# Cosine attention and a mixer MLP: score groups of three key chunks across pair borders, and three shared two-bank PSUM tiles

## The chip, the cores and the metric

The kernel runs on one core of a Trainium2 chip. The core has five engines that work side by side, each taking its own instructions in order: PE (the tensor engine; its weight loads are counted apart as PEld), ACT (activations), DVE (vector work), POOL (element work in on-chip memory, and the issue of some transfers) and SP (the issue of most transfers). Matmul results land in PSUM, which has eight banks of 512 fp32 columns on each of 128 partitions; ACT or DVE must move them out ("evict" them) before the place is used again. The metric is the device time of one execution in microseconds (us).

## The reference

Inputs are q, k and v of shape (8, 12, 448, 64): 8 batches, 12 heads, 448 tokens, 64 numbers a head.

```
q_n = q / (norm(q) + 1e-6);  k_n = k / (norm(k) + 1e-6)
scores = q_n @ k_n^T / tau                  # tau = 0.1
attn = softmax(scores)                      # over the keys
x = (attn @ v), heads side by side          # (8, 448, 768)
h = relu(x^T @ w_tok1) @ w_tok2             # 448 -> 256 -> 448, over tokens
u = x + h^T
out = u + relu(u @ w_ch1) @ w_ch2           # 768 -> 1536 -> 768, over channels
```

## The kernel before

The unit of the attention is a **pair** of heads; a batch has 6 pairs and the whole input 48, numbered i = 0 to 47. Keys are cut in 4 chunks of 112. For a pair the kernel does, in this order:

- `load_qk`, `load_v`: loads issued by SP, up to seven pairs ahead.
- `square`, `sums`, `norms`, `scale`: inverse norms of q and k and their product. Squares and products run on POOL (lines 187 and 221), the sums on DVE (L198, 1.2 us each), the logarithms and exponentials that make the inverse norm on ACT (L209 to L213). Later in the run `norms` is called once for three pairs.
- `tpose` (pairs 0 to 11, on PE, evicted by DVE at L237) or `tpose_dma` (pairs 12 and up, a transposing DMA from SP, L242): the transposed q and k, `qk`.
- `score(i, c)`: for key chunk c two matmuls (L256), one per head, each with 64 rows and 448 columns; the two heads lie on different halves of the array's rows and run together. They write the two banks of a tile `psS`, and ACT takes the exponential of both into `pt` (L258, 0.91 us).
- `pv(i, hh)`: 16 matmuls (L272) of `pt` with v and a column of ones into `psO`; DVE makes the reciprocal (L275) and the product `x` (L276).
- `tok1`: 8 matmuls (L285) into `psR`, Relu on DVE into `rt` (L288). `tok2`: 8 matmuls (L299) into `psU`, on DVE the sum with x as `u16` (L302). The transposed `ut` follows by a transposing DMA (L305), or on PE (`upose`, `psT`, L311).

When a batch's six pairs are through, its channel MLP is done in **units**, fed one by one between the steps of the next batches' pairs:

- `m_ch1(b, ct)`, 12 a batch: 6 matmuls (L321) of 448 columns into `psG`, evicted with a Relu by ACT into `gt` (L324).
- `m_ch2(b, m, dh)`: 12 matmuls (L336) of 384 columns into `psF`, evicted by DVE, which adds u into `ost` (L340). There are 6 or 8 units in a batch: three or four blocks of tokens m, two halves dh of the output columns. For m = 3 two additions of 64 partitions each evict a unit. After dh = 1 SP issues the output's transfers (L353, L359).

PSUM before: the pool `ps` has four tiles of one bank each, tag "b", used in turn by psO, psR, psU, psT, pst (of `tpose`), psG, psF and the warming matmuls; the pool `ps2` has two tiles of two banks for psS alone. `pts` are two buffers of `pt`, for even and odd pairs.

The order of each engine's work is the order in which the program writes it (`tc.manual_schedule`). The start (pairs 0 to 6) is written out by hand, with `warm(n)` calls of n small matmuls (L249) that only keep PE running. From pair 7 on, one turn of the loop is: two score chunks of pair i; side work for later pairs; some units; `pv` of pair i - 1; loads; some units; the other two chunks of pair i; units; `tok1` of i - 1; units; `tok2` of i - 1. `feed` takes units off the queue by a budget made of estimated PE times (`ns`), shared over what is left of the batch.

The framework puts in the semaphore waits: an instruction waits until what it reads is written and what it overwrites is read.

Of the kernel before, what the change touches and what calls it, by code (L numbers as in the profile page):

```python
# [22 lines left out]
def kernel(  # L23
# [12 lines left out]
    nc = tc.nc  # L36
# [45 lines left out]
    ps = ctx.enter_context(tc.tile_pool(name="ps", bufs=4, space=bass.MemoryType.PSUM))  # L82
    ps2 = ctx.enter_context(tc.tile_pool(name="ps2", bufs=2, space=bass.MemoryType.PSUM))
# [52 lines left out]
    for i in range(2):  # L136
        pt = cst.tile([SC, 8 * S + 64], FP16, name=f"pt{i}")
        nc.gpsimd.memset(pt[:, 8 * S:8 * S + 64], 0.0)
        pts.append(pt)
# [40 lines left out]
    def square(i, a, act=False):  # L180
        if "sq" not in pipe[i]:
            pipe[i]["sq"] = nrm.tile([SC, 2, 2 * NCH, E], FP32, name=f"sq_{i}", tag="sq")
        src = side(i, a).rearrange("p g c e -> p (g c) e")
# [5 lines left out]
    def side(i, a):  # L189
        return pipe[i]["kq"[a]][:]  # L190
# [24 lines left out]
    def scale(i, a, eng=None):  # L215
# [5 lines left out]
        (eng or nc.gpsimd).tensor_tensor(out=st["kqn"][:, a].rearrange("p c g e -> p g c e"), in0=side(i, a),  # L221
# [23 lines left out]
    def warm(n):  # L245
        if "warm" not in pipe:
            pipe["warm"] = ps.tile([128, 128], FP32, name="warm", tag="b")
        for _ in range(n):
            nc.tensor.matmul(pipe["warm"][:], id16[:], id16[:], start=True, stop=True)  # L249

    def score(i, c):
# [6 lines left out]
        nc.scalar.activation(out=pts[i % 2][:, 2 * S * c:2 * S * (c + 1)].rearrange("p (h s) -> p h s", h=2),  # L258
                             in_=psS[0:SC, :, 0:S], func=AF.Exp, scale=inv_tau)

    def pv(i, hh):
# [7 lines left out]
        for m, lo in enumerate(windows(b)):  # L269
            for c in range(NCH):  # L270
                at = (2 * c + hh) * S + lo
                nc.tensor.matmul(psO[:, m, 0:E + 1], pts[i % 2][:, at:at + 128],  # L272
                                 vt[:, g, c, 0:E + 1], start=(c == 0), stop=(c == NCH - 1))
# [5 lines left out]
    def tok1(i):  # L279
        st = pipe[i]  # L280
        w1 = (0, 1, 2, 3) if (i // NPAIR) % 2 == 0 else (4, 0, 1, 2)
        psR = ps.tile([128, TT, 128], FP32, name=f"psR_{i}", tag="b")
# [7 lines left out]
    def tok2(i, pe=False):  # L290
# [5 lines left out]
        psU = ps.tile([128, 4, 128], FP32, name=f"psU_{i}", tag="b")  # L296
# [17 lines left out]
    def m_ch1(b, ct):  # L314
# [4 lines left out]
        psG = ps.tile([128, S], FP32, name=f"psG_{b}_{ct}", tag="b")  # L319
        for dt in range(DT):  # L320
            nc.tensor.matmul(psG[:], wc1t[:, dt, ct * 128:(ct + 1) * 128],  # L321
                             ut[b][:, dt].rearrange("p m s -> p (m s)")[:, lo:lo + S],
                             start=(dt == 0), stop=(dt == DT - 1))
        nc.scalar.activation(out=gt[:, ct, (b % 2) * S:(b % 2 + 1) * S], in_=psG[:], func=AF.Relu)  # L324

    ost = {}

    def m_ch2(b, m, dh):
        gt = gts[b // 2]
        lo = 384 if m == 3 else 128 * m + (b % 2) * 512  # L330
        if dh == 0:
            ost[0] = outp.tile([128, D], FP32, name=f"ost_{b}_{m}", tag="ost")
        o = ost[0]
        psF = ps.tile([128, DH], FP32, name=f"psF_{b}_{m}_{dh}", tag="b")
        for ct in range(CT):
            nc.tensor.matmul(psF[:], gt[:, ct, lo:lo + 128], wc2t[:, ct, dh * DH:(dh + 1) * DH],  # L336
                             start=(ct == 0), stop=(ct == CT - 1))

        def add(p0, p1, bb, slot):
            nc.vector.tensor_tensor(out=o[p0:p1, dh * DH:(dh + 1) * DH].rearrange("p (j e) -> p j e", j=3),  # L340
                                    in0=psF[p0:p1].rearrange("p (j e) -> p j e", j=3),
                                    in1=u16[bb][p0:p1, 3 * dh:3 * dh + 3, slot], op=ALU.add)

        if m < 3:
            add(0, 128, b, m + b % 2)
        else:
            add(0, 64, b - 1, 3)
            add(64, 128, b, 0)
        if dh == 1:
            if m < 3:  # L350
                r = 0
                for c, p0, p1 in pieces(*MAIN[m]):
                    nc.sync.dma_start(out=out[b].rearrange("(p c) d -> c p d", c=NCH)[c, p0:p1],  # L353
                                      in_=o[r:r + p1 - p0])
                    r += p1 - p0
            else:
                (c, p0, p1), = pieces(384, S)
                for bb, r in ((b - 1, 0), (b, 64)):
                    nc.sync.dma_start(out=out[bb].rearrange("(p c) d -> c p d", c=NCH)[c, p0:p1],  # L359
                                      in_=o[r:r + 64])  # L360
# [4 lines left out]
    def ch1_units(b):  # L365
        return [(ns(S, DT), lambda ct=ct: m_ch1(b, ct)) for ct in range(CT)]

    def ch2_units(b):
        return [(ns(DH, CT), lambda m=m, dh=dh: m_ch2(b, m, dh))
                for m in ((3, 0, 1, 2) if b == B - 1 else range(3 + b % 2)) for dh in range(NDH)]  # L370

    queue = []
    fed = [0.0]

    def feed(budget, least=0.0):
        fed[0] += budget
        done = 0.0
        while queue and (fed[0] > queue[0][0] / 2 or done < least):
# [3 lines left out]
            done += t  # L382
        return done
# [5 lines left out]
    with tc.manual_schedule():  # L389
# [25 lines left out]
        warm(40)  # L415
        tpose(0, 1, 2)
        warm(3)
        tpose(0, 0, 1)
        warm(5)
# [8 lines left out]
        warm(12)  # L428
# [3 lines left out]
        warm(12)  # L432
# [11 lines left out]
        for i in range(1, NP_ALL + 1):  # L444
            b, pj = i // NPAIR, i % NPAIR
            if i < NPAIR:
# [9 lines left out]
                if i >= 2:  # L456
                    tok1(i - 2)
# [8 lines left out]
                if i >= 2:  # L466
                    tok2(i - 2, pe=(i == NPAIR - 1))
                pv(i - 1, 1)
                score(i, 3)
                if i == 1:  # L470
                    warm(8)
# [14 lines left out]
            if i == NPAIR:  # L486
# [6 lines left out]
                tok1(i - 2)  # L493
# [8 lines left out]
                tok2(i - 2, pe=True)  # L502
# [4 lines left out]
            if i == NPAIR + 1:  # L507
                queue += ch1_units(b - 1)
            early = i < 12
            least = 0.0 if early else 1.0  # L510
            if pj == 0:
                if b >= 2:
# [84 lines left out]
```

## Time and profile before

| | us |
|---|---|
| median of three runs (lowest, highest) | 408.69 (408.58, 409.4) |
| the profiled execution's own time | 407.75 |
| its span, first to last instruction | 406.0 |
| PE busy | 389.1 |
| ACT busy | 240.8 |
| POOL busy | 218.5 |
| DVE busy | 206.4 |
| mean granted clock of PE | 0.982 |

A row of the profile names the source line, the engine, the operation and the tiles as written<-read. In the page's first part stand busy time, its share of the span and the number of instructions. The fourth part follows the chain of work that ended last backwards. A timeline row gives the start in us, the length in us, the engine and what it did, and in brackets the idle time before it with what ended it; equal instructions that follow each other are one row with a count. The length of a row of matmuls takes in the time until its last result is out, so the next row can start before it ends: the pace of PE is read from starts. A row of a stretch gives its bounds, its length, the busy time of the engines asked for (PE, PEld, DVE, ACT, POOL, or PE alone) with the number of instructions, the clock granted to PE as a part of full speed, the busy share of the DMA engines, and GB/s.

### The profile page before, as it was taken

What the parts mean: (1) busy time and instruction counts of PE and PEld (TensorE: products, weight loads), DVE (VectorE), ACT (ScalarE), POOL (GpSimd) and SP (SyncE); (2) the same over time, 40 slices, a digit from 0 to 9 for tenths busy, and PEclk for the clock granted to TensorE, in tenths of its full rate; (3) what the DMA queues carried; (4) which work ended last, traced back from release to release, by engine and by line L of the source; (5) the groups of instructions that cost most, each with busy time, mean ns of one, the idle gap of its engine ahead of it and who ended that gap; (6) DMA issues with size and microseconds to landing.
All of it is one profiled execution on the core that took longest, in us unless ns stands there. A gap on an engine that the chain in (4) does not pass through costs nothing.

```text
span 406.0 us, 10118 instructions
## 1 busy us (share of the span) xinstructions
PE 389.1 (96%) x4146; PEld 240.4 (59%) x4146; DVE 206.4 (51%) x441; ACT 240.8 (59%) x392; POOL 218.5 (54%) x257
## 2 busy tenths in 40 slices
PE   6978799999999999999999999999999999999995
PEld 5656566566555665656656655556655666655562
DVE  5767877655454466554555555635636345312031
ACT  5857789954676438773587437773588535521400
POOL 7797999948557480949175852949092800000000
PEclk9868999999999999999999999999999999999999
DMA  8999999978859786867759697978974433103022
GB/s 198 239 175 251 246 262 230 209 195 180 201 142 191 140 200 157 197 161 171 201 127 187 156 184 188 164 152 187 195 130 94 114 81 92 28 15 116 2 74 81
DMA packets 102590, 64.07 MB, mean 158 GB/s; under 512 B 61328, under 2 KB 98960, under 8 KB 102544
## 3 DMA queue, kind: packets, MB, share of 16 engines
q1 hardware_dynamic: 96928, 58.22, 64.0%
q0 software_dynamic: 5616, 5.21, 8.1%
q8 instruction: 32, 0.52, 0.6%
q14 instruction: 14, 0.11, 0.1%
HBM read 43.45 MB, written 11.01 MB: 134 GB/s over the span
## 4 chain that ended last, share of the span: by engine, by line
PE 87%; DMA 5%; DVE 4%; POOL 1%; issue 1%; ACT 1%; SPq 0%; DVEq 0%; POOLq 0%
PE psF L336 27%; PE psG L321 27%; PE psO L272 12%; PE psS L256 10%; PE psU L299 5%; PE psR L285 5%; DMA kf<-in_k_dram 4%; DVE ssq L198 2%; DMA qf<-in_q_dram 1%; DVE x L276 1%; PE pst L235 1%; POOL kq L221 0%; ACT sq L185 0%; DVE ost L340 0%; DVE rt L288 0%
## 5 line engine op out<-in xcount | busy, mean ns | idle before, releaser
L258 ACT ACTIVATE pt<-psS 112x896 f16<-112x896 f32 x192 | 166.2, 914 | 84.4 <-PE psS L256 84.1
L321 PE MATMUL psG<-ut,wc1t 128*128 128x448 f16 x576 | 122.4, 353 | 0.0
L336 PE MATMUL psF<-wc2t,gt 128*128 128x384 f16 x672 | 116.6, 326 | 0.0
L221 POOL TENSOR_TENSOR kq<-kf,rn 112x512 f16<-112x512 f32 x47 | 50.0, 1063 | 99.3 <-ACT rn L213 86.3
L336 PEld LDWEIGHTS <-gt 128*128 128x128 f16 x672 | 63.1, 98 | 43.4 <-issue 5.2
L340 DVE TENSOR_TENSOR ost<-psF,u 128x384 f32<-128x384 f32 (+1 forms) x64 | 35.7, 557 | 96.2 <-PE psF L336 96.0
L324 ACT ACTIVATE gt<-psG 128x448 f16<-128x448 f32 x96 | 52.3, 545 | 53.7 <-PE psG L321 53.5
L321 PEld LDWEIGHTS <-wc1t 128*128 128x128 f16 x576 | 51.3, 98 | 46.6 <-issue 8.2
L198 DVE TENSOR_REDUCE ssq<-sq 112x16 f32<-112x1024 f32 (+1 forms) x49 | 58.1, 1189 | 9.0 <-ACT sq L185 6.4
L272 PEld LDWEIGHTS <-pt 112*128 112x128 f16 x1536 | 53.5, 99 | 15.5 <-ACT gt L324 7.0
L256 PE MATMUL psS<-qk 64*128 64x448 f16 x384 | 56.2, 363 | 3.5 <-ACT pt L258 2.7
L272 PE MATMUL psO<-vt,pt 112*128 112x65 f16 x1536 | 59.3, 195 | 0.1
L302 DVE TENSOR_TENSOR u<-psU,x 128x512 f16<-128x512 f32 x48 | 33.1, 689 | 34.2 <-PE psU L299 34.2
L187 POOL TENSOR_TENSOR sq<-kf 112x512 f32<-112x512 f32 x46 | 47.7, 1037 | 3.9 <-DMA kf<-in_k_dram 3.4
L221 POOL TENSOR_TENSOR kq<-qf,rn 112x512 f16<-112x512 f32 x45 | 46.8, 1041 | 0.0
L288 DVE TENSOR_SCALAR rt<-psR 128x256 f16<-128x256 f32 x48 | 20.2, 421 | 46.8 <-PE psR L285 46.6
L276 DVE TENSOR_TENSOR x<-psO,rec 128x256 f16<-128x256 f32 x96 | 40.8, 425 | 3.3
L187 POOL TENSOR_TENSOR sq<-qf 112x512 f32<-112x512 f32 x39 | 40.5, 1037 | 0.0
L285 PE MATMUL psR<-x,w1t 128*128 128x128 f16 x384 | 29.8, 221 | 2.6 <-DVE x L276 2.6
L285 PEld LDWEIGHTS <-w1t 128*128 128x128 f16 x384 | 25.0, 99 | 11.6 <-issue 3.3
L299 PEld LDWEIGHTS <-w2t 128*128 128x128 f16 x384 | 25.9, 100 | 9.0 <-issue 2.1
L299 PE MATMUL psU<-rt,w2t 128*128 128x128 f16 x384 | 30.1, 223 | 0.4 <-DVE rt L288 0.2
(40 smaller groups left out, 156.0 us busy)
## 6 DMA issues: line engine op xcount, KB each, us to landing
qf<-in_q_dram SPq DMA_DIRECT2D x48, 224.0 KB, 3.8
kf<-in_k_dram SPq DMA_DIRECT2D x48, 224.0 KB, 3.7
vf<-in_v_dram SPq DMA_DIRECT2D x48, 224.0 KB, 3.7
out_dram<-ost SPq DMA_DIRECT2D x8, 336.0 KB, 3.1
wc1t<-in_moe_w_ch_dram POOLq DMA_DIRECT2D x4, 576.0 KB, 8.2
wc2t<-in_moe_w_ch_dram POOLq DMA_DIRECT2D x2, 1152.0 KB, 16.3
out_dram<-ost SPq DMA_DIRECT2D x8, 288.0 KB, 2.9
out_dram<-ost SPq DMA_DIRECT2D x8, 240.0 KB, 2.8
```

Of the source, the lines that this page charges most:

```text
L187: nc.gpsimd.tensor_mul(out=pipe[i]["sq"][:, a], in0=src, in1=src)
L198: nc.vector.tensor_reduce(out=half[i // HP]["ssq"][:, a0:a1, lo:lo + 2 * NCH], in_=pipe[i]["sq"][:, a0:a1], axis=AXX.X, op=ALU.add)
L221: (eng or nc.gpsimd).tensor_tensor(out=st["kqn"][:, a].rearrange("p c g e -> p g c e"), in0=side(i, a), in1=_bcast_free(rn, E), op=ALU.mult)
L256: nc.tensor.matmul(psS[:, hh, 0:S], qk[hb:hb + 64, c * SC:c * SC + 128], qk[hb:hb + 64, S:2 * S], start=True, stop=True)
L258: nc.scalar.activation(out=pts[i % 2][:, 2 * S * c:2 * S * (c + 1)].rearrange("p (h s) -> p h s", h=2), in_=psS[0:SC, :, 0:S], func=AF.Exp ...
L272: nc.tensor.matmul(psO[:, m, 0:E + 1], pts[i % 2][:, at:at + 128], vt[:, g, c, 0:E + 1], start=(c == 0), stop=(c == NCH - 1))
L276: nc.vector.tensor_tensor(out=st["x"][:, :, hh * E:(hh + 1) * E], in0=psO[:, :, 0:E], in1=_bcast_free(rec[:], E), op=ALU.mult)
L285: nc.tensor.matmul(psR[:, tt], w1t[:, w1[m], tt * 128:(tt + 1) * 128], st["x"][:, m], start=(m == 0), stop=(m == 3))
L299: nc.tensor.matmul(psU[:, m], w2t[:, tt, lo:lo + 128], st["rt"][:, tt], start=(tt == 0), stop=(tt == TT - 1))
L321: nc.tensor.matmul(psG[:], wc1t[:, dt, ct * 128:(ct + 1) * 128], ut[b][:, dt].rearrange("p m s -> p (m s)")[:, lo:lo + S], start=(dt == 0) ...
L324: nc.scalar.activation(out=gt[:, ct, (b % 2) * S:(b % 2 + 1) * S], in_=psG[:], func=AF.Relu)
L336: nc.tensor.matmul(psF[:], gt[:, ct, lo:lo + 128], wc2t[:, ct, dh * DH:(dh + 1) * DH], start=(ct == 0), stop=(ct == CT - 1))
```

## The change

From pair 7 on the key chunks of all pairs form one list that is cut in groups of three, whatever pair they belong to: a group may hold the last chunk of one pair and the first two of the next. After each group the program writes the side work of the pairs that begin in it (`side(i)`), then one of `pv`, `tok1` or `tok2` of what is ready, then `feed`, then the `tok2` and `tok1` that may follow. Eight groups make a batch; `feed` gives each an eighth of the batch's units and at least one from the second batch on. `pt` has three buffers.

PSUM becomes three two-bank tiles (`ps2`, tag "s"), shared by psS, psG and psF, and in the start by psR, psU and some warming matmuls (`wide`), and two one-bank tiles (`ps`).

A unit of the channel MLP is twice as large: `m_ch1` makes two blocks ct in the two banks of one tile (one block in batch 0), each with its own Relu after its 6 matmuls, and `m_ch2` makes both halves dh in the two banks of one tile, each with its own addition after its 12 matmuls.

In the start, `warm(12)` before `sums(2)` goes, another becomes `warm(14)`, and `warm(8)` stands at the end of each of the pairs 1 to 5 and not of pair 1 alone.

```
-    ps = ctx.enter_context(tc.tile_pool(name="ps", bufs=4, space=bass.MemoryType.PSUM))
-    ps2 = ctx.enter_context(tc.tile_pool(name="ps2", bufs=2, space=bass.MemoryType.PSUM))
+    ps = ctx.enter_context(tc.tile_pool(name="ps", bufs=2, space=bass.MemoryType.PSUM))
+    ps2 = ctx.enter_context(tc.tile_pool(name="ps2", bufs=3, space=bass.MemoryType.PSUM))
...
-    for i in range(2):
+    for i in range(3):
         pt = cst.tile([SC, 8 * S + 64], FP16, name=f"pt{i}")
...
-    def m_ch1(b, ct):
+    def m_ch1(b, ct, n):
...
-        psG = ps.tile([128, S], FP32, name=f"psG_{b}_{ct}", tag="b")
-        for dt in range(DT):
-            nc.tensor.matmul(psG[:], wc1t[:, dt, ct * 128:(ct + 1) * 128],
-                             ut[b][:, dt].rearrange("p m s -> p (m s)")[:, lo:lo + S],
-                             start=(dt == 0), stop=(dt == DT - 1))
-        nc.scalar.activation(out=gt[:, ct, (b % 2) * S:(b % 2 + 1) * S], in_=psG[:], func=AF.Relu)
+        psG = ps2.tile([128, 2, 512], FP32, name=f"psG_{b}_{ct}", tag="s")
+        for j in range(n):
+            for dt in range(DT):
+                nc.tensor.matmul(psG[:, j, 0:S], wc1t[:, dt, (ct + j) * 128:(ct + j + 1) * 128],
+                                 ut[b][:, dt].rearrange("p m s -> p (m s)")[:, lo:lo + S],
+                                 start=(dt == 0), stop=(dt == DT - 1))
+            nc.scalar.activation(out=gt[:, ct + j, (b % 2) * S:(b % 2 + 1) * S], in_=psG[:, j, 0:S], func=AF.Relu)
...
+    def m_ch2(b, m):
...
+        psF = ps2.tile([128, 2, 512], FP32, name=f"psF_{b}_{m}", tag="s")
+        def add(dh, p0, p1, bb, slot):
+            nc.vector.tensor_tensor(out=o[p0:p1, dh * DH:(dh + 1) * DH].rearrange("p (j e) -> p j e", j=3),
+                                    in0=psF[p0:p1, dh, 0:DH].rearrange("p (j e) -> p j e", j=3),
+                                    in1=u16[bb][p0:p1, 3 * dh:3 * dh + 3, slot], op=ALU.add)
+
+        for dh in range(NDH):
+            for ct in range(CT):
+                nc.tensor.matmul(psF[:, dh, 0:DH], gt[:, ct, lo:lo + 128], wc2t[:, ct, dh * DH:(dh + 1) * DH],
+                                 start=(ct == 0), stop=(ct == CT - 1))
+            if m < 3:
+                add(dh, 0, 128, b, m + b % 2)
+            else:
+                add(dh, 0, 64, b - 1, 3)
+                add(dh, 64, 128, b, 0)
...
+    def feed():
+        fed[0] += fed[1]
+        done = 0
+        while queue and (done < fed[2] or fed[0] > queue[0][0] / 2):
+            t, fn = queue.pop(0)
+            fn()
+            fed[0] -= t
+            done += 1
+
+    def refill(b):
+        while queue:
+            queue.pop(0)[1]()
+        queue.extend((ch2_units(b - 1) if 0 < b < B - 1 else []) + ch1_units(b))
+        fed[:] = [0.0, sum(t for t, _ in queue) / 8, min(b, 1)]
+        if b == B - 2:
+            queue.extend(ch2_units(b))
...
-        warm(12)
         sums(2)
         cast_v(0)
         score(0, 2)
-        warm(12)
+        warm(14)
...
-                if i == 1:
-                    warm(8)
+                warm(8)
...
+        chunks = [(i, c) for i in range(NPAIR + 1, NP_ALL) for c in range(NCH)]
+        groups = [chunks[j:j + 3] for j in range(0, len(chunks), 3)]
...
+        while u_next < NP_ALL:
+            grp = groups[g] if g < len(groups) else []
+            for i, c in grp:
+                score(i, c)
+                if c == NCH - 1:
+                    seen[i] = g
...
+            begun = [i for i, c in grp if c == 0]
+            for i in begun:
+                side(i)
+            r_ok, u_ok = p_next, r_next
+            if seen.get(p_next, g) < g:
+                pv(p_next, 0)
+                pv(p_next, 1)
+                p_next += 1
+                r_ok = p_next
+            elif r_next < p_next:
+                tok1(r_next)
+                r_next += 1
+                u_ok = r_next
+            elif u_next < r_next:
+                tok2_of(u_next)
+                u_next += 1
+            feed()
+            for i in begun:
+                if i + 1 < DMA_T0:
+                    tpose(i + 1)
+            while u_next < u_ok:
+                tok2_of(u_next)
+                u_next += 1
+            while r_next < r_ok:
+                tok1(r_next)
+                r_next += 1
+            g += 1
```

`side(i)` holds the loads, sums, norms, products, squares, transposing DMA and cast that the loop before had in each turn, in the same order among themselves.

## The prediction

> **What bounds the kernel now.** I read the page first, then busy time by stretches, the tensor engine's timeline in one steady pair, the list of waits, and the clock in short stretches.
>
> ```profile
> PE 389.1 (96%) x4146; PEld 240.4 (59%) x4146; DVE 206.4 (51%) x441; ACT 240.8 (59%) x392; POOL 218.5 (54%) x257
> ...
> PE 87%; DMA 5%; DVE 4%; POOL 1%; issue 1%; ACT 1%; SPq 0%; DVEq 0%; POOLq 0%
> ```
>
> ```profile
> 84.00:372.00 288.00, 287.89 (x3042) 173.78 (x3041) 141.08 (x304) 168.06 (x259) 145.12 (x161) 1.00 0.67 149
> ```
>
> PE holds 87% of the chain, and from 84 to 372 us it is busy 287.89 of 288.00 us at full clock. There every microsecond that PE waits or saves is a microsecond of the end. ACT, DVE and POOL have slack.
>
> ```profile
> 273.99 0.61 PE L299 MATMUL psU<-rt,w2t 128*128 128x128 f16 x8
> 274.53 0.55 PE L256 MATMUL psS<-qk 64*128 64x448 f16 x4
> 275.01 1.19 PE L272 MATMUL psO<-vt,pt 112*128 112x65 f16 x32
> 276.05 2.11 PE L336 MATMUL psF<-wc2t,gt 128*128 128x384 f16 x12
> 278.09 0.55 PE L256 MATMUL psS<-qk 64*128 64x448 f16 x4
> 278.58 0.66 PE L336 MATMUL psF<-wc2t,gt 128*128 128x384 f16 x3
> ```
>
> Read the starts. psU takes 0.54 us before a score where it takes 0.45 before anything else (the chain gives psF 1.95, and 2.04 here before a score): entering a score group costs 0.10. Four score matmuls take 0.49; two concurrent pairs of 448 columns at psG's pace (1.14/6 = 0.19) are 0.38, so leaving costs 0.11. A group costs 0.21 us whatever its length.
>
> **Part 1, longer groups (gain).** Pairs 7 to 47 have 164 chunks: 82 groups of two before, 55 of three after. 27 x 0.21 = **-5.7 us**.
>
> **Part 2, MLP units on two-bank tiles (loss).** In batches 1 to 7 each unit holds two accumulations in one tile, j = 0 and 1, and the eviction of 0 stands before the matmuls of 1. The built instruction list, each wait followed to the instruction that brings its semaphore to the value, shows what this makes: the first matmul of half 1 of every psG waits for the Relu of half 0 of the same tile, and that of every psF for the add of half 0. Before, each unit had its own bank, and the list of waits has no PE row for L321 or L336. PE takes matmuls in order, so half 1, the psU and psR behind it and the next scores wait too, and with the scores ACT's exps, which have 41% of the span to give. There are 42 such psG and 28 psF units (3 or 4 a batch; batch 0's psG stay single). The trace shows this kind of bubble in psR to rt to psU:
>
> ```profile
> 48.29 0.62 PE L285 MATMUL psR<-x,w1t 128*128 128x128 f16 x8 [1.16 <-DVE x L276]
> 48.95 0.42 DVE L288 TENSOR_SCALAR rt<-psR 128x256 f16<-128x256 f32 x1
> 49.43 0.61 PE L299 MATMUL psU<-rt,w2t 128*128 128x128 f16 x8 [0.22 <-DVE rt L288]
> ```
>
> psR stops streaming at 48.74 (0.45 after its start), DVE starts 0.21 later, and PE resumes 0.06 after its end: the eviction plus 0.27.
> - psF: add 0.557 (L340) + 0.27 = 0.83, 24 times; the four m = 3 units need two adds (1.14 for both at 339.96): 1.41. 19.9 + 5.6 = 25.5.
> - psG with ACT free: Relu 0.545 (L324) + 0.27 = 0.81. ACT is not always free: from a group's start the first exp begins at +0.41 and the next every 0.80 (two and the row after them span 1.61 from 292.07), so three hold ACT to +2.81. With the projection (1.12) between, half 0 ends at 0.68 + 1.12 + 1.14 = 2.94 and finds ACT free: 28 units, 22.7.
> - In groups that hold only psU (0.45) before the unit, half 0 ends at 2.27; Relu runs from 2.81 to 3.36: 1.15, 6 times, 6.9.
> - In groups that begin a pair i with i mod 3 = 1, the four norm activations stand ahead of the Relu:
>
> ```profile
> 293.68 0.34 ACT L209 ACTIVATE rn<-ssq,tiny 112x48 f32<-112x48 f32 x1
> ...
> 294.84 0.53 ACT L324 ACTIVATE gt<-psG 128x448 f16<-128x448 f32 x1
> ```
>
> They take 1.16, so Relu starts at 3.97, and the bubble is 3.97 + 0.55 + 0.06 - 2.94 = 1.64, 8 times, 13.1.
>
> Sum of part 2: 25.5 + 22.7 + 6.9 + 13.1 = **+68.2 us**. Bounds: the evictions' bare durations, 24 x 0.557 + 4 x 1.14 + 42 x 0.545 = 40.8, if the 0.27 shrank to nothing; above, the sum with each bubble 0.2 larger, 82. I take 68, since the bubble row is the same mechanism.
>
> The Trainium skill speaks against such a wait: "PSUM — Partial Sum Buffer", Summary, says that PSUM may be read while a matmul runs if the matmul targets a different bank. The halves lie in different banks, so by that rule part 2 would cost nothing and the sum would end near 405.7. No run here shows it, and the program's waits decide.
>
> **Part 3, shared tiles.** Scores and MLP units rotate through three tiles, so a group's third chunk needs the tile of the last unit. Where psR or psU stands between (0.45 and more), its second eviction is done. Twelve groups (third chunks of 12_0, 15_0, 18_0 and every third pair to 45_0) follow a unit directly: tile free 0.81 after the unit, chunk ready at 0.10 + 0.38 = 0.48. 12 x 0.33 = **+4.0** (0 to 8, with an exp ahead of the Relu). psO, psR and psU have two banks for four: psO follows psR by a group's 0.78, which covers the eviction (0.42 + 0.27); cost nothing, or 0.3 a pair if DVE's 1.2 us sums get ahead.
>
> **Part 4, order.** psR 47 to psU 47 now touch: one bubble, +0.7. psR 12 waits for x behind psU 11 alone: +0.5. psT, norms, casts and loads keep their order on POOL, ACT and SP; per pair the same two loads, one transposing DMA and v load, moved behind three scores. Transposed keys (3.4 us to land) are issued about two groups ahead, some 10 us: covered. kq 10 is the exception: POOL ends it at 62.7, PE would ask near 61.3, +1.4; against it the waits behind DVE's double sums (0.51 at 66.28, 0.90 at 78.37) go: net 0, +-1.4. The third pt buffer only removes a reuse; its memset on POOL stands after the identity and before weights first used at 19.8.
>
> **Part 5, start and clock.** Full or half clock changes at steps of 3.41 us:
>
> ```profile
> 19.31:22.73 3.42, 1.80 (x30) 1.00 1.14 233
> 22.73:26.14 3.41, 3.12 (x32) 0.50 0.77 161
> 26.14:29.55 3.41, 2.77 (x29) 0.50 1.16 137
> 29.55:32.97 3.42, 3.42 (x41) 0.50 1.20 254
> 32.97:36.38 3.41, 2.58 (x40) 1.00 1.29 216
> 46.62:50.03 3.41, 2.03 (x28) 1.00 1.20 275
> ```
>
> Column three is PE busy, then the clock. It falls after 1.80 of 3.42 busy, stays after 2.03, and comes back only after a full stretch. warm(8), now in pairs 1 to 5 (8 x 0.056 at full clock, beside ACT's 4.6 us a pair), fills the gap at 26.4 to 27.4, so full clock returns at 29.55, 3.4 us earlier: **-1.5** (bounds -3 and +1). The removed warm(12) lies under key loads that land at 18.84: nothing.
>
> Later, a 1.64 bubble leaves 3.41 - 1.57 = 1.84 busy, nearer the 1.80 that fell than the 2.03 that held. The stretch must hold all of it: (3.41 - 1.6)/3.41 = 0.53 of 8, and about six in ten of those, 2.5 falls at 1.7 to 3.4 us each: **+5** (0 to 27). The other bubbles leave over 2.2. "TensorE: Matmul & The Clock Gate", Part 1, lets the clock fall after an idle window of 3.4 us; no bubble here is that long, so by it this term is 0. The row above fell half busy, so I go by the row.
>
> **Sum.** -5.7 + 68.2 + 4.0 + 1.2 + 0 - 1.5 + 5 = +71.2. The profiled execution took 407.75 (span 406.0 and 1.75 around it), so 479.0; the three runs' median lies 0.94 above that execution, which makes 480 for a median.
>
> **Rivals.**
> A: the halves run through (a wait satisfied early, or not where I read it). -5.7 + 4.0 + 1.2 - 1.5 = -2.0: 406.7, faster. For it: the banks differ and DVE and ACT are 51% and 59% busy. Against: a half can't be evicted before it ends, and PE takes matmuls in order. It decides below 2.0/70 = 0.03 us a unit, where the smallest eviction takes 0.545. 4%.
> B: bubbles as short as the bare evictions, no falls of the clock: 40.8 - 2.0 = +38.8 to about +55: 447 to 463. 14%.
> C: the clock falls at most long bubbles and takes two stretches to return, or ACT's queue makes all psG bubbles like the long ones (28 x 0.83 = 23 more): 500 to 515. For it: coming back needs 3.41 us without a gap, and units bring a gap every 2 to 4. 14%.
>
> **How the numbers follow.** Forecast 480, own range 463 to 497, 68%. With the upper half of B (455 to 463) and the near end of C (to 502) that makes 80%: 455 to 502. A change within 0.2% is about what a measurement can't tell from none. Only A is not slower: faster 0.04, same 0.01, slower 0.95.
>
> **What would show it.** PE waits on the DVE add and the ACT Relu, about 70 rows of 0.8 to 1.6 us and 60 to 75 us in sum, PE busy under 87%; psS starts in groups of six matmuls 0.68 long; a wait of psS on the add or Relu of 0.3; full clock again near 29.6; stretches at half clock after pairs 16, 19, 25. If PE has no wait inside psG or psF I am wrong altogether; if the bubbles are there and the time is under 455, their size is.

## The result, and the profile after

The changed kernel takes **482.05 us** in the median (480.67 to 484.08) where the kernel before takes 409.04 on the same chip: a ratio of 1.178, with a 95% interval of 1.173 to 1.184. The prediction was 480, with 455 to 502 as its range. The profiled execution took 483.31 us, its span 481.5. An execution that took over 1.5% more than the fastest one of its kernel is left out of the ratios.

The page of the changed kernel, first the busy times, then the shares of the chain that ended last:

```profile
PE 401.0 (83%) x4168; PEld 246.0 (51%) x4168; DVE 205.7 (43%) x441; ACT 241.9 (50%) x392; POOL 218.4 (45%) x258
...
PE 62%; ACT 15%; DMA 8%; DVE 7%; POOL 4%; issue 2%; SPq 0%; POOLq 0%
```

PE has fallen from 96% to 83% busy. On the chain ACT went from 1% to 15% and DVE from 4% to 7%, though both do the same work as before: 241.9 and 205.7 us against 240.8 and 206.4. They have become what PE waits for.

The list of waits, PE alone, from 88 us to the end (waiter, what it waited for: sum, times, longest):

```profile
PE psG L321 <- ACT gt L324: 34.3, 42, 1.6
PE psF L338 <- DVE ost L332: 20.4, 28, 1.2
PE psU L298 <- DVE rt L287: 2.7, 4, 0.7
PE psS L255 <- DVE ost L332: 1.0, 6, 0.2
PE psU L298 <- DVE x L275: 0.6, 1, 0.6
```

Before, the same list had no PE row in this part of the run. The counts of the first two rows are those of the instruction list: 42 psG units and 28 psF units wait once each, 54.7 us in sum. The list leaves out idle times under 0.15 us. The idle time is counted from the modelled end of the last matmul, which lies about 0.16 after the array could have taken the next one (a psG row is 1.30 long where its pace is 1.135), so PE loses 54.7 + 70 x 0.16 = 65.9 us of its stream.

The timeline, PE and ACT, near the end, where only units are left:

```profile
442.95 0.54 ACT L324 ACTIVATE gt<-psG 128x448 f16<-128x448 f32 x1 [0.59 <-PE psG L321]
443.54 2.43 PE L321 MATMUL psG<-ut,wc1t 128*128 128x448 f16 x12 [0.63 <-ACT gt L324]
...
444.87 0.54 ACT L324 ACTIVATE gt<-psG 128x448 f16<-128x448 f32 x1 [1.38 <-PE psG L321]
446.01 0.54 ACT L324 ACTIVATE gt<-psG 128x448 f16<-128x448 f32 x1 [0.59 <-PE psG L321]
446.60 2.43 PE L321 MATMUL psG<-ut,wc1t 128*128 128x448 f16 x12 [0.63 <-ACT gt L324]
```

Each row of 12 matmuls is half 1 of one unit and half 0 of the next. It starts 0.05 after the Relu of the half before has ended, and the rows follow each other every 3.06 us where two halves take 2.27: 0.79 lost a unit. The Relu at 444.87 belongs to the first half of the row at 443.54 and runs beside its second half: PE writes another tile there and does not stop. It stops only where the tile is the same.

Where ACT has the norms of three pairs to do first, the same view shows the long form:

```profile
142.10 1.30 PE L321 MATMUL psG<-ut,wc1t 128*128 128x448 f16 x6
...
143.21 0.34 ACT L209 ACTIVATE rn<-ssq,tiny 112x48 f32<-112x48 f32 x1
...
144.23 0.24 ACT L213 ACTIVATE rn<-rn 112x48 f32<-112x48 f32 x1
144.38 0.53 ACT L324 ACTIVATE gt<-psG 128x448 f16<-128x448 f32 x1
144.95 1.29 PE L321 MATMUL psG<-ut,wc1t 128*128 128x448 f16 x6 [1.56 <-ACT gt L324]
```

The half is through at 143.24 (1.14 after its start), its Relu starts 1.14 later, behind four small activations, and PE stands for 1.56 + 0.16 = 1.72.

The stretches from 44 to 90 us hold the second loss. First the kernel before (bounds, length, busy PE, PEld, DVE, ACT, POOL, PE's clock, DMA share, GB/s):

```profile
44.00:56.00 12.00, 10.49 (x159) 7.58 (x157) 9.70 (x22) 8.54 (x16) 11.04 (x13) 1.00 1.16 283
56.00:72.00 16.00, 15.49 (x213) 9.90 (x210) 12.01 (x24) 15.03 (x34) 15.70 (x18) 1.00 1.20 219
72.00:90.00 18.00, 17.10 (x188) 10.49 (x186) 9.52 (x20) 12.66 (x24) 13.27 (x15) 1.00 1.00 216
```

and the changed kernel:

```profile
44.00:56.00 12.00, 8.95 (x102) 5.09 (x99) 6.53 (x12) 7.88 (x16) 8.32 (x10) 1.00 1.14 236
56.00:72.00 16.00, 14.17 (x172) 8.77 (x173) 8.20 (x16) 10.88 (x22) 16.00 (x17) 0.79 1.15 226
72.00:90.00 18.00, 14.86 (x179) 9.32 (x176) 9.68 (x22) 14.57 (x29) 14.78 (x17) 1.00 1.14 241
```

The changed kernel is earlier at 44 us: its first scores of pair 7 start at 44.35 where they stood at 49.97 before. Then POOL idles for 3.7 of the 12 us to 56 and is full after it, PE is busy 2.2 us less in the last stretch, and the clock is down to 0.79 in between. The list of waits of POOL in the first 100 us says what it lacked; the first row is of the kernel before, the second of the changed one:

```profile
POOL sq L187 <- DMA kf<-in_k_dram: 3.0, 2, 1.8
```

```profile
POOL sq L187 <- DMA kf<-in_k_dram: 8.6, 4, 4.7
```

To put a number on this stretch I count the PE work done by a point in time: the matmuls that have started by then, each at its steady pace (psG 0.19, psF 0.1625, psS 0.1225, those of psR, psU, psT and pst 0.056, psO 0.032 us; warming matmuls nothing). By 44 us the kernel before has done 18.5 us and the changed one 22.0; by 90 us it is 59.9 and 55.0. A lead of 3.5 became a lag of 4.9. The measure is used again below; the figures in the expectations, written from an earlier count, differ by up to 1.4.

### The profile page after: what moved, and what is told of

It is laid out like the page before. It is cut to its first block, busy times and chain, and to the rows that moved or that the text cites. A ratio compares the mean times of both kernels' runs of the same rounds, so it can differ in the third digit from the quotient of the medians.

```text
span 481.5 us, 10090 instructions
## 1 busy us (share of the span) xinstructions
PE 401.0 (83%) x4168; PEld 246.0 (51%) x4168; DVE 205.7 (43%) x441; ACT 241.9 (50%) x392; POOL 218.4 (45%) x258
## 4 chain that ended last, share of the span: by engine, by line
PE 62%; ACT 15%; DMA 8%; DVE 7%; POOL 4%; issue 2%; SPq 0%; POOLq 0%
PE psF L338 24%; PE psG L321 19%; ACT pt L257 7%; PE psO L271 7%; ACT gt L324 5%; PE psS L255 5%; DVE ost L332 5%; DMA kf<-in_k_dram 4%; PE psU L298 3%; PE psR L284 3%; DMA qf<-in_q_dram 3%; POOL kq L221 2%; POOL sq L187 2%; DMA qk<-kq 2%; ACT rn L212 1%
## 5 line engine op out<-in xcount | busy, mean ns | idle before, releaser
L257 ACT ACTIVATE pt<-psS 112x896 f16<-112x896 f32 x192 | 163.1, 916 | 114.0 <-PE psS L255 113.8
L338 PE MATMUL psF<-wc2t,gt 128*128 128x384 f16 x672 | 117.4, 326 | 20.7 <-DVE ost L332 20.4
L321 PEld LDWEIGHTS <-wc1t 128*128 128x128 f16 x576 | 54.4, 98 | 89.1 <-issue 47.0
L338 PEld LDWEIGHTS <-gt 128*128 128x128 f16 x672 | 64.5, 97 | 67.0 <-issue 27.8
L255 PE MATMUL psS<-qk 64*128 64x448 f16 x384 | 52.9, 360 | 5.1 <-DMA qk<-kq 1.4
L298 PEld LDWEIGHTS <-w2t 128*128 128x128 f16 x384 | 24.4, 98 | 14.4 <-issue 8.1
L274 DVE RECIPROCAL rec<-psO 128x4 f32<-128x4 f32 x96 | 16.8, 176 | 32.3 <-PE psO L271 32.2
## 6 DMA issues: line engine op xcount, KB each, us to landing
wc2t<-in_moe_w_ch_dram POOLq DMA_DIRECT2D x2, 1152.0 KB, 18.5
```

Source lines behind the costliest of these rows:

```text
L255: nc.tensor.matmul(psS[:, hh, 0:S], qk[hb:hb + 64, c * SC:c * SC + 128], qk[hb:hb + 64, S:2 * S], start=True, stop=True)
L257: nc.scalar.activation(out=pts[i % 3][:, 2 * S * c:2 * S * (c + 1)].rearrange("p (h s) -> p h s", h=2), in_=psS[0:SC, :, 0:S], func=AF.Exp ...
L298: nc.tensor.matmul(psU[:, m], w2t[:, tt, lo:lo + 128], st["rt"][:, tt], start=(tt == 0), stop=(tt == TT - 1))
L321: nc.tensor.matmul(psG[:, j, 0:S], wc1t[:, dt, (ct + j) * 128:(ct + j + 1) * 128], ut[b][:, dt].rearrange("p m s -> p (m s)")[:, lo:lo + S ...
L338: nc.tensor.matmul(psF[:, dh, 0:DH], gt[:, ct, lo:lo + 128], wc2t[:, ct, dh * DH:(dh + 1) * DH], start=(ct == 0), stop=(ct == CT - 1))
```

## Theories, and the experiments

Theory 1: PE waits inside a unit because its two halves share a tile, and the wait is for the tile, for as long as the eviction takes. Rivals: ACT and DVE are late whatever the tiles; or PE can't write one bank while another is read. Theory 2, for the 44 to 90 us: the earlier arrival is worth nothing, because POOL and the key loads set the pace. Rivals: the arrival is kept; or the new order of the pairs 7 to 11 alone is at fault. Theory 3, for the rest: groups of three save what they should, and steps that touch give it back.

### Own tiles for each half

```
-        psG = ps2.tile([128, 2, 512], FP32, name=f"psG_{b}_{ct}", tag="s")
         for j in range(n):
+            psG = ps2.tile([128, 2, 512], FP32, name=f"psG_{b}_{ct + j}", tag="s")
...
-        psF = ps2.tile([128, 2, 512], FP32, name=f"psF_{b}_{m}", tag="s")
         for dh in range(NDH):
+            psF = ps2.tile([128, 2, 512], FP32, name=f"psF_{b}_{m}_{dh}", tag="s")
```

> Each half of a unit gets a two-bank tile of its own from the same three, and uses one bank of it; order of the instructions, pools and groups stay as in the changed kernel. Theory (PE waits inside a unit because both halves stand in one tile, and the wait is for the tile): the 70 waits, 54.7 us of idle time and about 0.16 of drain each, 66 us in all, go, while the evictions still read one bank as PE writes another: 482 - 66 = 416 (411 to 423), no PE row of psG or psF behind the Relu or the add above 3 us in sum. Rival 1 (the evictions come too late because ACT and DVE are behind their own queues, whatever the tiles): waits of the same sum move to the reuse of one of the three tiles, over 450. Rival 2 (PE and the evicting engine can't work in two banks at once): matmuls slow down beside the evictions and the time stays over 450 without wait rows.

Measured: 418.6 us (414.55 to 421.1) over four executions; ratio to the kernel before 1.020 (1.013 to 1.027), taken over three of them with a median of 417.12, which is used below. 64.9 of the 73 us are gone. The waits of PE from 92 us on, and PE with ACT in one feed of two units:

```profile
PE psU L298 <- DVE rt L287: 2.7, 4, 0.7
PE psS L255 <- DVE ost L331: 1.0, 6, 0.2
PE psU L298 <- DVE x L275: 0.6, 1, 0.6
```

```profile
130.12 4.70 PE L321 MATMUL psG<-ut,wc1t 128*128 128x448 f16 x24
...
131.45 0.54 ACT L324 ACTIVATE gt<-psG 128x448 f16<-128x448 f32 x1
...
132.59 0.54 ACT L324 ACTIVATE gt<-psG 128x448 f16<-128x448 f32 x1 [0.59 <-PE psG L321]
133.72 0.54 ACT L324 ACTIVATE gt<-psG 128x448 f16<-128x448 f32 x1 [0.59 <-PE psG L321]
...
134.66 0.61 PE L298 MATMUL psU<-rt,w2t 128*128 128x128 f16 x8
```

Not one psG or psF wait is left. Four halves run through in 134.66 - 130.12 = 4.54, four times 1.135, while ACT reads the tiles that PE has just left. Both rivals fall: the evictions are in time, and PE writes one bank while another is read. That is the rule of "PSUM — Partial Sum Buffer", Summary, in the Trainium skill, which the prediction set against the program's waits: of the hardware this run agrees with it, and so did the kernel before, where each unit's eviction ran beside matmuls in other banks and PE had no wait in the list. But a wait that the program holds by tile costs the time all the same.

### Own tiles for psG alone

The same edit in `m_ch1` only.

> Own tiles for the halves of psG alone; psF stays as in the changed kernel. Theory: the 42 waits of psG go (34.3 us idle + 42 x 0.16 = 41.0), the 28 of psF stay (20.4 + 28 x 0.16 = 24.9): 482 - 41 = 441 (437 to 447). Rival (one of the two kinds hides behind the other, or ACT's queue moves the wait from psG to the scores): over 450, or psF waits well above 20.4.

Measured: 440.73 us (439.47 to 443.84), ratio 1.079 (1.074 to 1.084). The psG rows are gone and the psF row is the same to the digit:

```profile
PE psF L338 <- DVE ost L332: 20.4, 28, 1.2
```

So psG costs 482.05 - 440.73 = 41.3 (expected 41.0) and psF 440.73 - 417.12 = 23.6 (expected 24.9). They don't hide behind each other.

### One tile, both evictions after both halves

```
         for j in range(n):
             for dt in range(DT):
...
+        for j in range(n):
             nc.scalar.activation(out=gt[:, ct + j, (b % 2) * S:(b % 2 + 1) * S], in_=psG[:, j, 0:S], func=AF.Relu)
```

and the same for the additions in `m_ch2`.

> Both halves stay in one tile, but both evictions are written after the matmuls of both halves. Theory: no wait inside a unit (-66); the tile comes free later, by two evictions (1.1) + 0.27 = 1.37 after the unit's end where the changed kernel's was 0.81. A group's third chunk wants that tile 0.48 after the group's start: 12 groups that follow a unit directly wait 0.9, and some 35 with psU or psR between (0.45) wait 0.3 to 0.45: 10.8 + 13 = 24 instead of 2, so 482 - 66 + 22 = 438 (422 to 445). Rival (the third chunk's wait is as small as measured, 0.17, because PE enters the group later than I count): 416 to 420. Rival 2 (waits inside a unit are not by tile): no change from 482.

Measured: 433.5 us (432.74 to 435.87), ratio 1.061 (1.056 to 1.066). The waits inside a unit are gone with the tile still shared, so it is the eviction that stands between the halves that makes them. The price is paid at the third chunk of the next group:

```profile
PE psS L255 <- DVE ost L333: 8.4, 15, 1.0
PE psS L255 <- ACT gt L325: 2.9, 5, 0.6
```

The list has 20 waits of 11.3 us; five more of 0.13 to 0.14 in the same place are too short for it. Together they are 12.0, or 16.0 with 0.16 each, where I had 47 waits of 24: those behind a psU or psR are covered. They make up the 16.4 over the run with own tiles.

### One eviction twice as long

```
-            nc.scalar.activation(out=gt[:, ct + j, (b % 2) * S:(b % 2 + 1) * S], in_=psG[:, j, 0:S], func=AF.Relu)
+            for _ in range(n - j):
+                nc.scalar.activation(out=gt[:, ct + j, (b % 2) * S:(b % 2 + 1) * S], in_=psG[:, j, 0:S], func=AF.Relu)
```

> The changed kernel with the Relu of half 0 of each psG (batches 1 to 7) written twice in a row, so that this one eviction takes 1.09 us instead of 0.545. Theory (half 1 waits for the whole eviction of half 0, so the bubble is its length plus a fixed part): each of the 42 waits grows by 0.545, 22.9 in all: 482 + 23 = 505 (500 to 509), the psG waits 34.3 + 22.9 = 57 in sum, and the 28 psF waits stay at 20.4. Rival (the wait is for the first write of the tile alone, or a fixed latency, not the eviction's length): 480 to 487.

Measured: 510.84 us (508.68 to 511.97), ratio 1.248 (1.245 to 1.252).

```profile
PE psG L321 <- ACT gt L325: 58.6, 42, 2.1
PE psF L339 <- DVE ost L333: 20.4, 28, 1.2
```

The ordinary psG bubble went from 0.63 to 1.21 idle, the long one from 1.55 to 2.13: +0.58 each, 24.3 in sum where I had 22.9. The bubble is the eviction's length plus a fixed part. The rest of the 28.8 is the clock. In stretches of PE (bounds, length, busy, clock, DMA, GB/s) of this run:

```profile
234.35:237.77 3.42, 1.28 (x6) 0.92 0.48 142
237.77:241.18 3.41, 3.41 (x25) 0.58 0.49 75
...
323.10:326.51 3.41, 1.27 (x8) 1.00 0.57 158
```

Three times (the others at 265.07 and 384.54) a stretch with 1.27 to 1.39 busy is followed by one near half speed; each costs (0.08 + 0.42) x 3.41 = 1.7, so 5.1, and 24.3 + 5.1 = 29.4. The last row is one that held with as little.

### The start without the added warm(8)

With own tiles:

```
                 score(i, 3)
-                warm(8)
+                if i == 1:
+                    warm(8)
```

> The kernel with own tiles for each half (first run of this set), with the warm(8) at the ends of the pairs 2 to 5 taken out again, as before the change (pair 1 keeps it). Theory (key loads and POOL set the pace from 45 to 86 us, so PE's earlier arrival at pair 7, 44.35 instead of 49.97, is given back there): the same time as the first run of this set, within 1.5 us, with shorter waits of POOL on the key loads. Rival 1 (the earlier arrival is kept to the end): 3 to 6 us slower than the first run. Rival 2 (the early arrival does harm, by the waits that pull the clock down at 57 to 64 us): 2 to 5 us faster.

Measured: 417.74 us (416.76 to 420.56), ratio 1.023 (1.018 to 1.027): no difference from the 417.12 with it. PE has done 20.4 us of work by 44 us instead of 21.9, and 54.0 instead of 52.5 by 90 us; POOL's waits for keys fall from 10.9 to 5.9 us. The earlier arrival is given back, as theory 2 says.

### The start's warm(8) alone, in the kernel before

```
                 score(i, 3)
-                if i == 1:
-                    warm(8)
+                warm(8)
```

> The kernel before with one part of the change alone: warm(8) at the end of each of the pairs 1 to 5. Theory (from 45 to 86 us POOL and the key loads set the pace, so an earlier arrival of PE at pair 7 is given back): the time of the kernel before, -1.5 to +1 us, even where the clock stays up from 22.7 to 33. Rival (the earlier arrival, up to 5.6 us, is kept): 403 to 406.

Measured: 409.64 us (407.2 to 411.38), ratio 1.000 (0.997 to 1.004). The clock does stay up from 24 to 48 us, and the work done by 44 us rises from 18.5 to 22.4; by 90 us it is 56.8 against 59.9. The gain I had predicted for this part, -1.5, is not there.

But that the warm(8) is what keeps the clock up is not shown. The run with the weights alone (the last one below) has only the warm(8) of pair 1, and its program is that of the kernel before until the scores of pair 4 are done. Yet it held full clock where the profile of the kernel before had half, had 21.7 us of work done by 44 us, and came to pair 7 early. Its stretch, and the first scores of pair 7 in the kernel before and in that run:

```profile
22.73:26.14 3.41, 2.76 (x53) 1.00 1.08 182
```

```profile
49.97 0.61 PE L256 MATMUL psS<-qk 64*128 64x448 f16 x4
```

```profile
45.10 0.61 PE L256 MATMUL psS<-qk 64*128 64x448 f16 x4
```

So most of the lead in the profiles can be a difference between two executions of one start. The other executions of the kernel before on record have a mean clock of 0.985 to 1.0 where the profiled one has 0.982, and when they came to pair 7 is not known. What speaks for theory 2 is that the time doesn't follow the arrival: the profiled execution of the kernel before, at pair 7 by 49.97, took 407.75, the one with the weights alone, by 45.10, took 408.19, and the one with the warm(8), by 43.97, took 410.64.

### The old order for the pairs 7 to 11

With own tiles. The old turn of the loop, cut to its core, stands ahead of the groups, which begin with pair 12:

```
+        for i in range(NPAIR + 1, 12):
...
+            quota = sum(t for t, _ in queue) / (2 * NPAIR + 1 - i)
+            score(i, 0)
+            score(i, 1)
...
+            feed_by(quota * 0.22)
+            pv(i - 1, 0)
+            pv(i - 1, 1)
+            cast_v(i)
+            load_v(i + 4)
+            feed_by(quota * 0.28)
...
+            score(i, 2)
+            score(i, 3)
+            feed_by(quota * 0.25)
+            tok1(i - 1)
+            feed_by(quota * 0.25)
+            tok2(i - 1)
-        chunks = [(i, c) for i in range(NPAIR + 1, NP_ALL) for c in range(NCH)]
+        chunks = [(i, c) for i in range(12, NP_ALL) for c in range(NCH)]
```

> The kernel with own tiles for each half, with the pairs 7 to 11 written in the order of the kernel before (two chunks, side work, pv of the pair before, two chunks, tok1, tok2, with batch 0's units between by the old shares), and groups of three from pair 12 on. Counted as PE work done by 90 us, the kernel before has 59.7 us done, the changed one 53.7, the one with own tiles 51.1, though both led by 3 at 44 us. Theory (the order of the pairs 7 to 11 leaves PE with nothing to do while POOL makes the next keys; the old order has units and pv there): most of the 8.6 come back: 409 to 413, and PE busy over 14 of the 16 us from 48 to 64 us. Rival (the key loads and POOL set the pace of this stretch whatever the order): 416 to 420, PE busy under 13 of 16.

Measured: 414.69 us (412.39 to 417.92), ratio 1.014 (1.007 to 1.022), between the two ranges. The work done by 90 us came back from 52.5 to 58.9, but PE was busy 12.61 of the 16 us from 48 to 64, which is what the rival said, and POOL still waited 8.0 us for keys. Of the 6.4 us of work only 2.4 appear in the median, and the two intervals overlap. Nor is one profile enough: the changed kernel and its runs with own tiles, own tiles for psG alone, both evictions late and one eviction twice as long have the same program up to 90 us, and had 52.5 to 56.2 done by then; the old order had 58.9 here and 56.2 in the run with tok1 held back. So the order seems to matter, and the split between order and loads is not settled.

### Groups of two

With own tiles:

```
-        groups = [chunks[j:j + 3] for j in range(0, len(chunks), 3)]
+        groups = [chunks[j:j + 2] for j in range(0, len(chunks), 2)]
-        fed[:] = [0.0, sum(t for t, _ in queue) / 8, min(b, 1)]
+        fed[:] = [0.0, sum(t for t, _ in queue) / 12, min(b, 1)]
```

> The kernel with own tiles for each half, with groups of two chunks instead of three (82 groups), and each group fed a twelfth of a batch's units instead of an eighth. Theory (a group costs 0.21 us to enter and leave, whatever its length): 27 groups more cost 5.7; against it the waits of the third chunk (6 x 0.33) and the small gaps of psU and psF behind three exps (about 1.7) go: +2 over the 418.6 of groups of three, 419 to 423. Rival (what a longer group saves is all given back by its exps, which hold tiles and ACT): the same or faster, 412 to 417.

Measured: 426.93 us (424.23 to 430.04), ratio 1.044 (1.037 to 1.050): 9.8 slower than groups of three (417.12), where I had +2. The waits of PE from 92 us on:

```profile
PE psR L284 <- DVE x L275: 6.9, 8, 0.9
PE psU L298 <- DVE rt L287: 2.8, 4, 0.8
PE psO L271 <- ACT pt L257: 1.2, 5, 0.2
```

In shorter groups tok1 stands right behind its own pv: 10.9 us of waits where groups of three have 4.3. From 90 us to its last matmul this run takes 327.4 us, with 59.7 of work done before; the run with groups of three 323.3 with 52.5 done. That is 11.3 for the steady part, near the 12.3 that 27 x 0.21 and 6.6 more of listed waits make; gaps too short for the list stand in both and are not in this sum.

### tok1 held back where no pv follows

With the kernel with own tiles and the old order for the pairs 7 to 11:

```
-            while r_next < r_ok:
-                tok1(r_next)
-                r_next += 1
+            if seen.get(p_next, g + 1) <= g:
+                while r_next < r_ok:
+                    tok1(r_next)
+                    r_next += 1
```

> The kernel with own tiles and the old order for the pairs 7 to 11 (414.69), with one change of order from pair 12 on: tok1 is not written at the end of a group when the next group has no pv to do; it stands after that group's scores, a unit after it, then tok2. Before, such a group (two in eight) ran scores, psU, unit, and the next scores touched the unit. Theory (the steady stretch loses what the longer groups save because steps that need each other touch: psU behind rt 4 x 0.69, third chunk 3 x 0.46 and 6 x 0.17, and 0.16 of drain for each of 14): these 5.4 + 2.2 go, 414.7 - 7.6 = 407 (405 to 410), no PE wait from 92 us on above 0.5. Rival (the waits only move, to psR behind x or psO behind pt): 413 to 416.

Measured: 416.29 us (413.01 to 418.57), ratio 1.017 (1.014 to 1.021): no faster. The waits did go, 5.4 to 1.5 in sum, and from 90 us to the last matmul the profiled run takes the same 317.8 us as the run before it, with 2.7 us less work done beforehand. But part of the wait only moved to where the list doesn't show it: eleven times psR takes 0.70 before a unit instead of 0.45, which fits a first half that takes the tile the first exp still reads, and six score groups are followed 0.44 later. And by 90 us this run had 56.2 done where the other had 58.9, though the two programs are the same until pair 12. Its stretch from 44 to 90 us just went worse.

### Weights loaded later

In that kernel, and in the kernel before with the warm(8):

```
-                else:
+                elif i < 4:
                     weights_ch1(i - 2)
...
-            if i == 8:
+            if i in (7, 8):
+                weights_ch1(i - 5)
+            if i == 9:
                 weights_ch2()
```

> The kernel of the run before this one in the set, with 1.2 MB of weights taken out of the time before 44 us: the third and fourth parts of wc1t are loaded in the pairs 7 and 8 instead of 4 and 5, and wc2t in pair 9 instead of 8. Theory (key loads that share the DMA engines with the weights hold POOL, which waits 8.0 us for keys before 56 us, and POOL holds PE): POOL's waits on keys fall to under 4 and the time by 2 to 4 us: 403 to 406. Rival (POOL ends its work at 85 us whatever waits it had, since ACT and DVE are in its chain too): within 1 us of the run before.

Measured: 414.2 us (412.02 to 416.2), ratio 1.012 (1.009 to 1.016), 2.1 under the run before it, not the 403 to 406 of the theory. The lead does grow (39.5 us of work by 64 us, against 36.5), and then PE stands at the first transposing DMA:

```profile
PE psS L255 <- DMA qk<-kq: 6.9, 1, 6.9
```

POOL's waits for keys fell only from 8.6 to 6.6. What the transposed keys of pair 12 waited for in their turn was not tried.

> The kernel before with warm(8) in the pairs 1 to 5 (409.64) and the weights loaded later as in the run before this one in the set. Theory (key loads were the limit that took the earlier start back): 404 to 407. Rival (as there): 408.5 to 410.5.

Measured: **406.94 us** (405.99 to 409.12), ratio 0.9955 (0.9933 to 0.9977): 1.8 us faster than the kernel before, and the fastest of all. POOL waits 3.2 us for keys where the warm(8) alone had 4.9, and 60.8 us of work are done by 90 us, where the kernel before has 59.9.

The weights alone, in the kernel before without the added warm(8):

> The kernel before with the weights loaded later alone (third and fourth parts of wc1t in the pairs 7 and 8, wc2t in pair 9), without the warm(8) of the pairs 2 to 5. The two together gave 406.94, the warm(8) alone 409.64, the kernel before 408.8. Theory (the earlier start is worth something only where the keys come early enough, so both are needed): 408 to 409.5. Rival (the later weights give the whole 2.7 by themselves, PE's earlier arrival nothing): 405.5 to 407.

Measured: 409.09 us (407.56 to 410.31), ratio 0.998 (0.996 to 1.001). Neither half of the edit is a gain by itself that can be told from nothing, and both together are 0.45%. Their ratios multiply to 0.9988; the distance to 0.9955 is 0.0033, which the three intervals (together about 0.0045) allow by chance, so that each needs the other is not shown.

## Why the prediction was right, and where it was not

- **Part 2, bubbles.** Right in cause, number and size. I had 68.2; the trace has 65.9, and taking the shared tiles away gave 64.9. psF: 24 of 0.81 and 4 of 1.37 are 24.9 (25.5 predicted). psG: 31 of 0.79, 3 of 0.91 and 8 of 1.71 are 40.9 (42.7 predicted). The step that was off is the group of 1.15 behind psU alone: six were predicted, three of 0.91 came. The eight behind the norms are there, at 1.71 for 1.64.
- **Part 1, groups.** The price of a group holds: six score matmuls take 0.67 to 0.68 to the next row, four 0.48 to 0.49, and psR in front of them 0.54 for 0.45. With listed waits counted apart, groups of two cost about what 27 x 0.21 says. But the saving of 5.7 doesn't reach the end, since the same order brings the losses of the next point, 9.9.
- **Part 3 and 4.** I had 4.0 for twelve third chunks and 1.2 for psU and psR. The third chunks are right: the list has six of 0.17, and five more stand at 0.147, below what it shows. With the 0.16 that is 0.33 and 0.31 each, 3.5 in sum (the twelfth, of pair 12, waits for its transposed keys instead). One of the five is inside this row of six matmuls, 1.07 long where one without a wait is 0.74, and 1.00 from the next row where that one is 0.67:

```profile
125.95 1.07 PE L255 MATMUL psS<-qk 64*128 64x448 f16 x6
```

  The step that failed is the other one: five psU waits are 3.3 (4.1 with the 0.16) where I had 1.2. To these come gaps that I had at nothing: psU to the unit behind it 0.64 or more for 0.45 nine times, and psU 0.06 later behind a group of three eight times, 2.3. Together 9.9 instead of 5.2.
- **Part 5, start.** Here the working failed, twice over. I expected the clock to come back 3.4 us sooner and to keep 1.5. In fact it never fell at 22.73, and PE came to pair 7 5.6 us sooner; and none of it was kept. First, I took the fall in one profile of the kernel before for a fixed part of its time: the run with the weights alone had no fall there without any added warm(8). Second, I carried a gain on PE before 44 us to the end, while in the next stretch POOL waits for the key loads, and PE for POOL. By 90 us the changed kernel is 4.9 us behind, where I had 1.5 ahead. The runs without and with the warm(8) show no difference in either kernel; that the order of the pairs 7 to 11 makes the lag is supported by the work done at 90 us (56.2 and 58.9 with the old order, 52.5 to 56.2 with the new) and not shown.
- **Part 5, clock.** Predicted +5 for falls behind the long bubbles. There were none: PE has full clock from 88 us on. The rule that I drew from two rows, that a stretch falls at 1.80 busy and holds at 2.03, put 1.84 on the wrong side. The changed kernel has six stretches with 1.85 to 1.89 busy, all at full clock; two of them:

```profile
142.20:145.61 3.41, 1.85 (x12) 1.00 0.68 161
...
196.81:200.22 3.41, 1.86 (x23) 1.00 0.66 172
```

- **The sum.** The profiled execution is 75.6 above the one before (483.31 - 407.75), and I had 71.2. The misses are -2.3 (bubbles), +6.4 (start), -5 (clock), +4.7 (parts 3 and 4), 3.8 in sum of the 4.4; the 0.6 left over are not traced. So the large term was right, and that the 480 is good to half a per cent is luck: the errors of the small terms went against each other.
- **What would show it.** Of the signs that I named, the 70 rows, their sum (with the 0.16), PE under 87% and the score groups of 0.68 are there. The third chunk's wait of 0.3 is there eleven times of twelve. Two signs are false: the clock has no return near 29.6 because it never fell there, and no half-clock stretches stand after pairs 16, 19 and 25.
- **The rivals.** A, the halves run through, falls by the 70 rows. B needed bubbles of the bare evictions: 0.79 against 0.545 for psG. C needed falls of the clock or an ACT that is always late; neither came, though the run with the longer Relu shows the falls a little further on.

## What to carry to other kernels

Count the program's waits per tile, not per bank: two accumulations in one PSUM tile, with the eviction of the first written between them, put the eviction and about a quarter of a microsecond on the path of PE once a unit, however idle the evicting engine is. A tile of its own for each accumulation takes the whole of it away, with nothing else changed; both evictions behind both accumulations take most of it. And before an earlier start is booked as a gain, look at the next stretch for the engine that is full there and for what it waits for: here an arrival about 5 us earlier left nothing in the time, and the one kernel that came out faster had also moved 1.2 MB of weights out of the way of the key loads. And one profile shows one execution: see whether a gap that you mean to fill stands in a second one.

## What was not expected of the hardware

The clock is not told by the busy share of a stretch alone. Six stretches with 1.85 to 1.89 of 3.41 us busy kept full clock, where one with 1.80 had lost it; with longer evictions three with 1.27 to 1.39 busy lost it and one with 1.27 and one with 1.43 did not. "TensorE: Matmul & The Clock Gate", Part 1, speaks of an idle window of 3.4 us; no gap in these stretches is listed with more than 2.14, and the clock fell all the same. What decides it stays open.

The stretch from 44 to 90 us does not repeat. Two kernels with the same program up to pair 12 had 58.9 and 56.2 us of PE work done by 90 us, five others, with one program up to there, 52.5 to 56.2, and the times of one changed kernel lay about 3 to 6.5 us apart from execution to execution. Differences of 2 or 3 us between two kernels that touch this stretch, as those of the runs with the old order, tok1 held back and the later weights, can be read only from many executions or from the profile of the part behind it.
